# Block sums of w_out on one engine, and low parts of a weight and of a few rows moved off VectorE, in an attention and two-MoE kernel

## The chip, the cores and the metric

The kernel runs on one core of a Trainium2 chip. The metric is the device time of one execution in microseconds (us). The median of three runs of the kernel before is 1247.25 us (1245.92 to 1251.09).

## The reference

Attention over 4 batches of 8 heads, 576 positions and 64 columns, with a bias that a small network computes from the positions; its output, 2304 rows of 512, goes through a gated layer of width 1536 (the first MoE) and then through a squared-relu layer of width 2048 (the second MoE). All data are float32 or wider.

```python
scores = scale * np.matmul(q, k.transpose(0, 1, 3, 2))
...
return np.matmul(attn, v).astype(np.float32)

def _moe_ref(x, w_gate, w_val, w_out) -> np.ndarray:
    g = x @ w_gate
    silu = g * (1.0 / (1.0 + np.exp(-g)))
    val = x @ w_val
    return (silu * val @ w_out).astype(np.float32)

def _moe2_ref(x, w_in, w_out) -> np.ndarray:
    h = np.maximum(x @ w_in, 0.0)
    return (h * h @ w_out).astype(np.float32)
```

## The kernel before

Every product is made of float16 parts: a number is written as a high part and a low part, and three matmuls (high by high, high by low, low by high) stand for one. Making parts is the work of ScalarE, VectorE and GpSimd. `halves` (L194) does it for a scaled input in one of four ways. In way 0 ScalarE writes the high part and VectorE the low part (`minus`, L191). In way 1 GpSimd writes the high part (L197) and VectorE the low part. In way 2 ScalarE scales the input in place (L205) and copies the high part (L209), and GpSimd subtracts for the low part (`rest_of`, L220). The table `MIX` (L30) lists for each kind of work which ways take turns; `mixed(key)` deals out the next. `diff` (L1192) is a sum or difference on VectorE for 0 and on GpSimd otherwise, and `parts2` (L1195) makes a high part (way 0 VectorE, 1 ScalarE, 2 GpSimd) and then a low part with `diff`.

The 2304 rows are nine units of 256. The first MoE takes them one by one (`moe1`, m from 0 to 8): gate and value products for 12 slices of the width (L458), `th` (L466 to L469), then the output product (L481) and `out_y` (L490), which scales the two halves of 128 rows, splits them into a high and a low part in the tile `yh` and stores them to DRAM through SP's queue (L502). The second MoE reads them back transposed.

Beside the last units of the first MoE the weights of the second are prepared (`weights2`, L1236). `first` decodes columns 2 and 3 of w_in (columns 0 and 1 were done earlier), finds a scale for each, and calls `split` (L286) four times for each; `second` does the same for the 16 blocks of w_out (key "2"), with a norm on ScalarE (L361) in between.

The second MoE treats unit 0 alone (`plain`, L1386) and the others as four pairs (`hidden`, `outputs`). For a pair, the eight blocks of rows of w_out are multiplied by the seven-product scheme of Strassen in Winograd's form: seven products in place of eight, for which sums and differences of blocks are needed on both sides. The sums of the hidden rows are made by GpSimd in `hidden` (key "s", tile `zx`). Those of w_out's blocks are made once, by `combine(f)` (L1206) for f from 0 to 7: seven differences into the tile `w2t` (three of 128x512, four of 128x256; L1220 to L1226, dealt out by key "t" as two on VectorE, one on GpSimd), then a high part on ScalarE (key "c") and a low part on VectorE or GpSimd (key "d": 0, 1, 1) into `TS[f]`. All eight use the one buffer `w2t`. Blocks 0 to 2 are called at the end of `weights2`; block 3 in `plain` behind f = 1, 4 behind f = 3, 5 behind f = 5, 6 behind f = 7, and 7 in front of the output products (L1403), of which there are two for 128 rows each, 48 matmuls each, going through f from 0 to 7.

In `hidden`, TensorE makes two products of 12 matmuls for each f (L1375) into banks of a pool of five; ScalarE reads a bank with relu (L1380) and squares (L1384), GpSimd makes four sums, and `parts2` makes the parts, which `outputs` (L1434) multiplies (L1447). In `outputs`, sums of the products are kept in small tiles c1, u2, u4, u3 with two buffers each, in the pool `wk`.

The order of the instructions on each engine is not that of the program. A planner in the compiler simulates the engines with its own costs and lets each engine take, of what is ready, what comes first in the program; what stands under `high_priority` goes ahead. On the chip each engine keeps the order thus found. Two generators, attention with the weights and the first MoE, are interleaved by hand-set positions (`LEAD`, L37).

Of the kernel before, what the change touches and what calls it, by code (L numbers as in the profile page):

```python
# [10 lines left out]
F32 = mybir.dt.float32  # L11
# [4 lines left out]
AF = mybir.ActivationFunctionType  # L16
ALU = mybir.AluOpType
# [7 lines left out]
P = 128  # L25
# [4 lines left out]
MIX = {  # L30
# [4 lines left out]
}  # L35

# [39 lines left out]
def tile_attention_moe(  # L76
# [4 lines left out]
    nc = tc.nc  # L81
# [20 lines left out]
    st = {}  # L102
# [111 lines left out]
    def mixed(k):  # L214

        mix_n[k] = mix_n.get(k, -1) + 1
        return MIX[k][mix_n[k] % len(MIX[k])]

    def rest_of(out_, x, hi):
        nc.gpsimd.tensor_tensor(out=out_, in0=x, in1=hi, op=ALU.subtract)  # L220
# [65 lines left out]
    def split(ring, key, j, kc, sc):  # L286

        src = ring.whole(key, j, kc)
        hi, lo = [ring.parts(key, j, kc, l) for l in range(2)]
        halves(hi, lo, src, sc, mixed(key))  # L290

    def root_scale(m, mm):

# [126 lines left out]
    def junk_tile():  # L420
        return junk1
# [68 lines left out]
    def out_y(m, t, po, iu):  # L490
        ss = scr([P, 1], tag="yss")
        nc.scalar.activation(junk_tile()[:, 0:512], po, AF.Square, accum_out=ss)
        r = expo(ss, half=True)
        sy = scr([P, 1], tag="ysy")
        nc.vector.tensor_scalar(
            out=sy, in0=r[:, 1:2], scalar1=2.0 ** -50, scalar2=None, op0=ALU.mult)
        mul(ftok[:, 2 * m + t:2 * m + t + 1], r[:, 0:1], iu, 2.0 ** 49)
        yh = mw.tile([P, 2, DM], F16, tag="yh", name="yh", bufs=1)
        nc.scalar.activation(yh[:, 0, :], po, AF.Copy, scale=sy)
        nc.vector.scalar_tensor_tensor(  # L500
            out=yh[:, 1, :], in0=po, scalar=sy, in1=yh[:, 0, :], op0=ALU.mult, op1=ALU.subtract)
        nc.sync.dma_start(y_d[m][P * t:P * t + P, :], yh.rearrange("p l e -> p (l e)"))  # L502


# [701 lines left out]
    def combine(f):  # L1206

        q = st["w2r"].t.rearrange("p a b -> p (a b)").bitcast(F16).rearrange("p (s c) -> p s c", c=256)
        t = st["w2t"]
        tv = t.rearrange("p (a b c) -> p a b c", a=2, b=2)  # L1210
        t1, t2, t3, t4 = [t[:, 256 * i:256 * i + 256] for i in range(4)]
        a, b = 4 * (W2 + f), 4 * (W2 + 8 + f)

        def right(l):
            return q[:, a + 2 * l + 1:b + 2 * l + 2:32, :]

        def left(l):
            return q[:, a + 2 * l:a + 2 * l + 2, :]

        t13 = tv[:, :, 0, :]  # L1220
        diff(t13, right(0), left(0), mixed("t"))
        diff(t13, t13, right(1), mixed("t"), ALU.add)
        diff(t13, t13, left(1), mixed("t"))
        for x, c, y in ((t2, b + 1, t1), (t4, b, t2)):
            diff(x, q[:, c], y, mixed("t"))
            diff(x, x, q[:, c + 2], mixed("t"), ALU.add)  # L1226
        hi, lo = st["TS"][f]
        parts2(hi, lo, t, "c", "d")
# [7 lines left out]
    def weights2():  # L1236
        a_stack.close()
        w2p = ctx.enter_context(tc.tile_pool(name="w2p", bufs=2, side="right"))
        ps2 = ctx.enter_context(tc.tile_pool(name="ps2", bufs=5, space=PSUM))
        w2r = Ring(w2p.tile([P, 25, 512], F32, name="w2r", bufs=1), {  # L1240
            "w": lambda j, kc: (w2a, 4 * j + kc) if j < 2 else 4 * j - 8 + kc, "2": lambda j, kc: W2 + kc})
        st["w2p"], st["ps2"], st["w2r"] = w2p, ps2, w2r

        def mm2():
            return ps2.tile([P, 512], F32, tag="ph", name="mm2")

        w2s = w2p.tile([P, 3584], F32, name="w2s", bufs=1)
        sg2 = Stage(
            512, [w2s[:, 1024 * i:1024 * i + 1024].bitcast(I64) for i in range(3)],
            [w2s[:, 3072 + 256 * i:3328 + 256 * i].bitcast(BF16) for i in range(2)])  # L1250
        yield from first(w2r, {"w": w2i}, range(2, 4), block_rows, sg2, 3, mm2)
        kappa = []
        for j in range(4):
            kap = keep()
            mul(kap, st["iw", j], st["iw", j], KR)
            kappa.append(kap)
        yield from second(w2r, "2", NF2, w2o, kappa, sg2, 3, mm2, True)
        new = w2p.tile([P, 4096], F16, name="w2c", bufs=1)

        st["w2t"] = w2p.tile([P, 1024], F32, name="w2t", bufs=1)  # L1260
        w2h, wrh, w2sh = [t.rearrange("p a b -> p (a b)").bitcast(F16) for t in (
            w2r.t, wr.t, w2s.rearrange("p (a b) -> p a b", a=7))]
        rooms2 = [w2sh[:, 1024 * i:1024 * i + 1024] for i in range(7)] + [w2h[:, 1024 * 24:1024 * 25]] + [
            new[:, 1024 * i:1024 * i + 1024] for i in range(4)] + [
            wrh[:, 1024 * i:1024 * i + 1024] for i in (4, 5, 6, 36)]
        st["TS"] = [rooms2[2 * f:2 * f + 2] for f in range(8)]
        st["HS"] = [wrh[:, int(1024 * o):int(1024 * o) + 3584] for o in (7.5, 11, 15, 18.5, 22, 25.5, 29, 32.5)]
        st["yt"] = wrh[:, 0:4096]
        for f in range(3):
            if f == 1:  # L1270
                yield ("gv", 8)
                yt_load((0,))
            combine(f)
            yield 3.0
# [70 lines left out]


    wk = ctx.enter_context(tc.tile_pool(name="wk", bufs=2, side="left"))
    fac = res.tile([P, 18], F32, name="fac")
    nc.vector.tensor_scalar(out=fac, in0=ftok, scalar1=st["G1"], scalar2=None, op0=ALU.mult)
    mul(fac, fac, fac)  # L1350
# [83 lines left out]
    def outputs(us):  # L1434
        n = 256 * len(us)
        nh = n // 2
        last_bank = mm2()
        for t in range(nh // P):
            banks = [mm2(), mm2(), mm2()] if t else [ma(), mm(), mm()]
            (p1, p2), (p6, p7), (p5, p3) = [[bk[:, 256 * i:256 * i + 256] for i in range(2)] for bk in banks]  # L1440
            p4 = last_bank[:, 256 * t:256 * t + 256]

            def product(po, a, b, fs=range(8)):
                for f in fs:
                    for k, (l, wl) in enumerate(((0, 0), (0, 1), (1, 0))):
                        o = nh * (a - 1 + 7 * l) + P * t
                        nc.tensor.matmul(  # L1447
                            po, HS[f][:, o:o + P], right_of(f, wl, b),
                            start=f == 0 and k == 0, stop=f == 7 and k == 2)

            def sums(name):
                return wk.tile([P, 256], F32, tag=name, name=name)

            def add(name, x, y):
                o = sums(name)
                nc.vector.tensor_tensor(out=o, in0=x, in1=y, op=ALU.add)
                return o

            def row(j, h, src, other):

                i = nh * (1 - h) + P * t
                u, tt = us[i // 256], i % 256 // P
                sc = fac[:, 2 * u + tt:2 * u + tt + 1]
                o = obs[h][:, 256 * j:256 * j + 256]
                nc.vector.tensor_tensor(out=o, in0=src, in1=other, op=ALU.add)
                nc.scalar.activation(o, o, AF.Copy, scale=sc)

            obs = [wk.tile([P, DM], F32, tag="ob", name="ob", bufs=3) for _ in range(2)]
            early_, late_ = (range(6), range(6, 8)) if t == 0 else (range(8), ())
            for fs in (early_, late_):  # L1470
                for po, a, b in ((p1, A11, B11), (p6, S2, T2), (p5, S1, T1)):
                    product(po, a, b, fs)
            c1 = sums("c1")
            nc.scalar.copy(c1, p1)
            u2 = add("u2", p6, c1)
            u4 = add("u4", p5, u2)
            product(p7, S3, T3)
            u3 = add("u3", p7, u2)
            row(1, 1, p5, u3)
            product(p2, A12, B21)  # L1480
            row(0, 0, p2, c1)
            product(p3, S4, B22)
            row(1, 0, p3, u4)
            product(p4, A22, T4)
            row(0, 1, p4, u3)
            for h in range(2):
                i = nh * (1 - h) + P * t
                for p0, np_, r0 in out_rows(us[i // 256], i % 256 // P):
                    nc.sync.dma_start(out[r0:r0 + np_, :], obs[h][p0:p0 + np_, :])
# [37 lines left out]
```

## Time and profile before

| | |
|---|---|
| median of three runs | 1247.25 us |
| the profiled execution | 1241.6 us, its span 1239.8 us |
| mean granted TensorE clock | 0.954 of full speed |
| TensorE (PE) busy | 1099.7 us, 89% |
| VectorE (DVE) busy | 782.3 us, 63% |
| ScalarE (ACT) busy | 669.9 us, 54% |
| GpSimd (POOL) busy | 642.3 us, 52% |

A busy share says how long an engine worked in the span. A window shows the same for a stretch, with the granted clock (1.00 is 2.4 GHz) and the share of DMA. In a row of groups or of a timeline stand line, engine, operation, output and inputs with their shapes, and in brackets or behind a bar how long the engine stood idle before it and who ended that. A wait list adds such idle times up. L1193 is the line of `diff`, so its instructions are told apart by tile: w2t is a block sum of w_out, zx a sum of the hidden rows, wr a part of them (or of a block sum, wr<-w2t).

### The profile page before, as it was taken

To read this page: it belongs to the slowest core of one execution; us is meant where nothing else is said; L and a number is where in the kernel's file an instruction comes from. 1 tells how busy PE (TensorE), PEld (TensorE's weight loads), DVE (VectorE), ACT (ScalarE), POOL (GpSimd) and SP (SyncE) were. 2 spreads that over 40 slices of the span, in tenths; PEclk is the share of its full clock that TensorE was granted. 3 is DMA by queue.
4 is the path that set the end of the run, shared out by engine and by line. 5 is a ranking of instruction groups with operands and counts; after the bars stand their busy time and mean duration, and the time that the engine had idled before them with its cause. 6 is when DMAs were issued, how large, how long until landed. Compare 5 with 4: busy or idle time off the path is not lost. (4 is left out here: it accounts for less than half of the span.)

```text
span 1239.8 us, 27146 instructions
## 1 busy us (share of the span) xinstructions
PE 1099.7 (89%) x10478; PEld 811.3 (65%) x10478; DVE 782.3 (63%) x1866; ACT 669.9 (54%) x1350; POOL 642.3 (52%) x811
## 2 busy tenths in 40 slices
PE   2587799998678889999997999979998899999998
PEld 2566788686467578686774767556743756848657
DVE  5989857887676666666565745884757335153361
ACT  3567767557566566566563543365635245163451
POOL 2433213279768697778694462235567236062360
PEclk9779799999879999999999999989999899999999
DMA  8957543219999999998989994650201101002001
GB/s 220 266 134 208 177 132 87 50 58 201 220 214 209 217 218 169 230 184 170 182 170 247 240 228 129 213 176 10 43 17 23 30 18 35 35 1 52 19 1 35
DMA packets 278078, 163.20 MB, mean 132 GB/s; under 512 B 233276, under 2 KB 246588, under 8 KB 277948
## 3 DMA queue, kind: packets, MB, share of 16 engines
q1 hardware_dynamic: 277948, 161.46, 55.9%
q8 instruction: 82, 1.34, 0.5%
q14 instruction: 48, 0.39, 0.1%
HBM read 92.13 MB, written 19.48 MB: 90 GB/s over the span
## 5 line engine op out<-in xcount | busy, mean ns | idle before, releaser
L458 PEld LDWEIGHTS <-wr 128*128 128x128 f16 x2592 | 253.4, 100 | 50.7 <-issue 14.9
L1193 POOL TENSOR_TENSOR zx<-zx 128x256 f32<-128x256 f32 x128 | 123.3, 974 | 150.1 <-ACT zx L1384 145.4
L458 PE MATMUL mm<-xT,wr 128*128 128x256 f16 x1536 | 185.5, 276 | 7.9 <-DVE yh L500 3.4
L220 POOL TENSOR_TENSOR pt<-s,pt 128x512 f16<-128x512 f32 x224 | 173.1, 796 | 30.4 <-ACT pt L836 27.8
L1447 PEld LDWEIGHTS <-wr 128*128 128x128 f16 x1344 | 132.1, 99 | 23.8 <-ACT wr L1200 3.5
L220 POOL TENSOR_TENSOR zx<-th,zx 128x256 f16<-128x256 f32 x108 | 82.5, 765 | 123.7 <-ACT zx L443 117.6
L481 PE MATMUL mm<-wr,zx 128*128 128x512 f16 x612 | 143.1, 381 | 1.5 <-DVE sc L828 1.1
L1193 DVE TENSOR_TENSOR wr<-zx,wr 128x768 f16<-128x768 f32 (+2 forms) x72 | 93.3, 1302 | 66.6 <-ACT wr L1200 65.6
L821 DVE CUSTOM_DVE_ANT_0 s<-qk,room 128x576 f32<-128x576 f32 x144 | 107.8, 749 | 40.8 <-PE qk L812 24.0
L829 ACT ACTIVATE s<-s,sc 128x576 f32<-128x576 f32 x112 | 85.6, 771 | 56.1 <-DVE sc L828 48.9
L458 PE MATMUL mm<-zx,wr 128*128 128x256 f16 x864 | 105.1, 279 | 2.8 <-DVE th L469 1.5
L1375 PE MATMUL mm<-wr,room 128*128 128x512 f16 (+1 forms) x480 | 101.3, 361 | 4.6 <-ACT zx L1380 4.5
L481 PEld LDWEIGHTS <-zx 128*128 128x128 f16 x648 | 60.3, 98 | 66.4 <-issue 3.5
L604 DVE TENSOR_TENSOR scrap<-scrap,room 128x1024 f16<-128x1024 f16 (+1 forms) x108 | 85.1, 801 | 24.3 <-PE ma L643 20.6
L1375 PE MATMUL mm<-wr,w2r 128*128 128x512 f16 (+1 forms) x480 | 100.0, 358 | 0.0
L620 POOL TENSOR_TENSOR scrap<-scrap 128x256 f32<-128x256 f32 (+1 forms) x90 | 64.1, 712 | 64.7 <-ACT scrap L619 56.5
L874 PE MATMUL av<-vp,pT 128*128 128x65 f16 (+3 forms) x1792 | 70.8, 197 | 26.9 <-DMA pT<-pt 23.9
L874 PEld LDWEIGHTS <-pT 128*128 128x128 f16 (+1 forms) x1792 | 61.7, 103 | 42.3 <-DMA pT<-pt 33.0
L1375 PEld LDWEIGHTS <-room 128*128 128x128 f16 x480 | 47.2, 98 | 52.1 <-issue 7.5
L643 PEld LDWEIGHTS <-scrap 128*128 128x128 f16 x1440 | 60.0, 105 | 27.5 <-issue 11.9
L1375 PEld LDWEIGHTS <-w2r 128*128 128x128 f16 x480 | 47.0, 98 | 46.6
L812 PE MATMUL qk<-kp,qT 128*128 128x288 f16 x384 | 64.1, 293 | 11.4 <-DMA kp<-kT_d 6.1
(273 smaller groups left out, 2093.3 us busy)
## 6 DMA issues: line engine op xcount, KB each, us to landing
kp<-kT_d SPq DMA_DIRECT2D x64, 288.0 KB, 3.3
vp<-v_d SPq DMA_DIRECT2D x48, 325.0 KB, 3.6
w2s<-in_moe_w_out_dram SPq DMA_DIRECT2D x16, 512.0 KB, 4.1
wr<-in_moe_w_gate_dram SPq DMA_DIRECT2D x24, 256.0 KB, 4.8
wst<-in_moe_w_out_dram SPq DMA_DIRECT2D x12, 512.0 KB, 3.6
wr<-in_moe_w_val_dram SPq DMA_DIRECT2D x24, 256.0 KB, 4.2
v_d<-vp SPq DMA_DIRECT2D x16, 325.0 KB, 2.9
y_d<-yh SPq DMA_DIRECT2D x18, 256.0 KB, 3.4
```

The source lines that it names most:

```text
L220: nc.gpsimd.tensor_tensor(out=out_, in0=x, in1=hi, op=ALU.subtract)
L458: nc.tensor.matmul(pg[:, 256 * gi:256 * gi + 256], wr.parts(key, f // 4, cc, wl, P * (f % 4), P), mov(xl, cc), start=k == 0, stop=k == 11)
L481: nc.tensor.matmul(po, zall[:, f, zl, P * t:P * t + P], wr.parts("o", 0, f, wl), start=k == 0, stop=k == 3 * NF1 - 1)
L604: nc.vector.tensor_tensor(out=m[:, :, ni * e:ni * e + ni], in0=block(kb, i0, ni), in1=th, op=ALU.is_gt)
L620: nc.gpsimd.tensor_tensor(out=tmp[r], in0=tmp[r], in1=xb, op=ALU.mult)
L812: nc.tensor.matmul(pq[:, j, 0:288], qT[:, 2 * (n % 4) + s, :], kts[0][:, js], start=s == 0, stop=s == 1)
L821: nc.vector.tensor_tensor_reduce(out=s.rearrange("p (a j) -> p a j", a=2), in0=pq[:, :, 0:288], in1=bias[:, n].rearrange("p (a j) -> p a j ...
L829: nc.scalar.activation(s, s, AF.Exp, bias=nm, scale=-1.0)
L874: nc.tensor.matmul(av[r, slot, 0:cn], pT[:, 5 * l + c, r], vs[e][c][:, c0:c0 + cn], start=m == 0, stop=m == 13)
L1193: (nc.gpsimd if how else nc.vector).tensor_tensor(out=out_, in0=a, in1=b, op=op)
L1375: nc.tensor.matmul(ph[:, :n], w2r.parts("w", g // 4, cc, wl, P * (g % 4), P), yt[:, 4 * yl + cc, :], start=m == 0, stop=m == 11)
L1447: nc.tensor.matmul(po, HS[f][:, o:o + P], right_of(f, wl, b), start=f == 0 and k == 0, stop=f == 7 and k == 2)
```

## The change

It does four things. Key "t" deals out only VectorE, so that all 56 differences of `combine` are made there. `combine` takes its buffer from a list that goes round: one buffer, as before, in `weights2`, and three from `plain` on, the two halves of a new tile `four` in the pool `wk` and the old one; the small tiles of `outputs` go into the halves of `four` in turn, in place of their own. `split` uses way 2 for columns 2 and 3 of w_in, where ways 2, 0, 1 took turns over the eight calls. And for m = 7 and 8 `out_y` has ScalarE write the scaled rows in float32 to a scratch tile, ScalarE copy the high part, and GpSimd subtract for the low part.

```diff
-    "t": (0, 0, 1), "c": (1,), "d": (0, 1, 1), "q": (0,), "s": (1,), "a": (1, 1, 0),
+    "t": (0,), "c": (1,), "d": (0, 1, 1), "q": (0,), "s": (1,), "a": (1, 1, 0),
...
-        halves(hi, lo, src, sc, mixed(key))
+        halves(hi, lo, src, sc, 2 if key == "w" and j > 1 else mixed(key))
...
-        nc.scalar.activation(yh[:, 0, :], po, AF.Copy, scale=sy)
-        nc.vector.scalar_tensor_tensor(
-            out=yh[:, 1, :], in0=po, scalar=sy, in1=yh[:, 0, :], op0=ALU.mult, op1=ALU.subtract)
+        if m < 7:
+            nc.scalar.activation(yh[:, 0, :], po, AF.Copy, scale=sy)
+            nc.vector.scalar_tensor_tensor(
+                out=yh[:, 1, :], in0=po, scalar=sy, in1=yh[:, 0, :], op0=ALU.mult, op1=ALU.subtract)
+        else:
+            y = junk_tile().bitcast(F32)
+            nc.scalar.activation(y, po, AF.Copy, scale=sy)
+            nc.scalar.copy(yh[:, 0, :], y)
+            rest_of(yh[:, 1, :], y, yh[:, 0, :])
...
-        t = st["w2t"]
+        t = st["w2t"][0]
+        st["w2t"].append(st["w2t"].pop(0))
...
-        st["w2t"] = w2p.tile([P, 1024], F32, name="w2t", bufs=1)
+        st["w2t"] = [w2p.tile([P, 1024], F32, name="w2t", bufs=1)]
...
+    four = wk.tile([P, 2048], F32, name="four", bufs=1)
+    st["w2t"] = [four[:, 0:1024], four[:, 1024:2048]] + st["w2t"]
...
-            def sums(name):
-                return wk.tile([P, 256], F32, tag=name, name=name)
+            def sums(i):
+                return four[:, 1024 * (t % 2) + 256 * i:1024 * (t % 2) + 256 * i + 256]
...
-            c1 = sums("c1")
+            c1 = sums(0)
             nc.scalar.copy(c1, p1)
-            u2 = add("u2", p6, c1)
-            u4 = add("u4", p5, u2)
+            u2 = add(1, p6, c1)
+            u4 = add(2, p5, u2)
             product(p7, S3, T3)
-            u3 = add("u3", p7, u2)
+            u3 = add(3, p7, u2)
```

## Rows read from the trace of the kernel before

**Rows 1.** Windows of two pairs (engines' busy us, instructions, clock, DMA)

```profile
908.34:1001.34 93.00, 83.02 (x530) 52.60 (x529) 48.13 (x52) 36.31 (x56) 46.05 (x43) 0.94 0.08 21
1001.34:1079.46 78.12, 78.12 (x530) 51.65 (x528) 31.41 (x35) 34.03 (x53) 30.33 (x32) 1.00 0.10 28
```

**Rows 2.** Stage window: the last rows of the first MoE

```profile
805.80:840.00 34.20, 26.43 (x198) 20.98 (x197) 30.21 (x74) 22.36 (x56) 11.31 (x11) 0.85 0.51 161
```

**Rows 3.** TensorE's waits after 800 us (total us, times, longest)

```profile
PE mm L1375 <- ACT zx L1380: 4.5, 2, 3.2
PE ma L458 <- DVE th L469: 4.3, 1, 4.3
PE ma L1447 <- ACT wr L1200: 3.2, 1, 3.2
PE mm L131 <- DVE sc L495: 3.0, 1, 3.0
```

**Rows 4.** Window of the instructions on tile w2t alone

```profile
863.40:951.50 88.10, 31.14 (x41) 8.35 (x8) 30.59 (x23) 0.99 0.10 25
```

**Rows 5.** Waits between 868 and 1002 us, all engines

```profile
POOL w2t L1193 <- DVE w2t L1193: 16.9, 13, 3.7
```

**Rows 6.** ScalarE's timeline, first pair (start, us, instruction, idle before)

```profile
913.72 0.60 ACT L1380 ACTIVATE zx<-mm 128x512 f32<-128x512 f32 x1 [1.33 <-PE mm L1375]
918.38 1.04 ACT L1200 CAST w2c<-w2t 128x1024 f16<-128x1024 f32 x1 [4.06 <-POOL w2t L1193]
```

**Rows 7.** Tile w2t on VectorE (ns min/median/max), one timeline row

```profile
L1193 DVE TENSOR_TENSOR w2t<-w2r,w2t x11: 414/426/1367, 867.3 to 946.3; 128x256 f32<-128x256 f16 x11
L1193 DVE TENSOR_TENSOR w2t<-w2r x6: 676/692/1207, 863.5 to 937.7; 128x512 f32<-128x512 f16 x6
L1193 DVE TENSOR_TENSOR wr<-w2t,wr x1: 1218/1218/1218, 935.1 to 935.1; 128x1024 f16<-128x1024 f32 x1
946.26 0.93 DVE L1193 TENSOR_TENSOR w2t<-w2r,w2t 128x256 f32<-128x256 f16 x1 [0.56 <-POOL w2t L1193]
```

**Rows 8.** Groups on VectorE, 860 to 955 us (busy us, mean ns)

```profile
L1193 DVE TENSOR_TENSOR w2t<-w2t,w2r 128x512 f32<-128x512 f32 x10 | 8.4, 839 | 6.1 <-POOL w2t L1193 5.9
L1193 DVE TENSOR_TENSOR w2t<-w2t,w2r 128x256 f32<-128x256 f32 x11 | 6.9, 628 | 3.4 <-POOL w2t L1193 3.3
L1193 DVE TENSOR_TENSOR w2t<-w2r,w2t 128x256 f32<-128x256 f16 x11 | 6.6, 601 | 5.9 <-POOL w2t L1193 5.8
L1193 DVE TENSOR_TENSOR w2t<-w2r 128x512 f32<-128x512 f16 x6 | 5.2, 859 | 3.9 <-POOL w2s L1193 3.8
```

**Rows 9.** Tile yh: its stores, first and last issue, time to landing

```profile
L502 SPq DMA_DIRECT2D y_d<-yh x18: 337/343/934, 248.4 to 874.4; - x18
DMA to landing us min/median/max: 2.0/3.4/6.6
```

**Rows 10.** TensorE's timeline: the plain unit's products

```profile
887.62 20.88 PE L1403 MATMUL mm<-w2r,wr 128*128 128x512 f16 x96
```

**Rows 11.** Windows around 878 us; the first of tile wr alone

```profile
878.00:894.00 16.00, 16.00 (x119) 3.04 (x31) 6.97 (x9) 2.46 (x4) 0.00 (x0) 1.00 0.34 67
870.00:878.00 8.00, 8.00 (x76) 7.16 (x75) 7.65 (x15) 6.59 (x17) 5.35 (x5) 1.00 0.08 33
```

**Rows 12.** Groups of VectorE and ScalarE, 795 to 840 us

```profile
L191 DVE SCALAR_TENSOR_TENSOR w2r<-w2r,keep 128x512 f16<-128x512 f32 x5 | 4.1, 826 | 0.6 <-POOL w2r L197 0.6
L500 DVE SCALAR_TENSOR_TENSOR yh<-mm,sc,yh 128x512 f16<-128x512 f32 x2 | 1.5, 746 | 0.0
L262 DVE TENSOR_SCALAR w2r<-w2s 128x512 int32<-128x512 int32 x14 | 7.7, 552 | 4.4 <-DMA w2s<-in_moe_w_out_dram 4.3
811.90 0.75 DVE L191 SCALAR_TENSOR_TENSOR w2r<-w2r,keep 128x512 f16<-128x512 f32 x1 [0.59 <-POOL w2r L197]
L205 ACT ACTIVATE w2r<-w2r,keep 128x512 f32<-128x512 f32 x3 | 2.1, 716 | 4.0 <-DVE keep L296 4.0
L209 ACT CAST w2r<-w2r 128x512 f16<-128x512 f32 x3 | 1.8, 611 | 0.1
```

More of the change, by code (lines that the diff above doesn't have):

```diff
@@ L1449, in product, with add @@
                             start=f == 0 and k == 0, stop=f == 7 and k == 2)
-            def sums(name):
-                return wk.tile([P, 256], F32, tag=name, name=name)
-            def add(name, x, y):
-                o = sums(name)
+            def sums(i):
+                return four[:, 1024 * (t % 2) + 256 * i:1024 * (t % 2) + 256 * i + 256]
+            def add(i, x, y):
+                o = sums(i)
                 nc.vector.tensor_tensor(out=o, in0=x, in1=y, op=ALU.add)
```

## The prediction

> **What bounds the kernel now.** I read the slices of the page first, then the stage windows, then TensorE's waits, then the timelines of the stages with holes. TensorE is the busiest engine by far, so a change on the others can only pay where it stands still or runs at a lowered clock. The second pair of units of the second MoE shows a stretch with no loss: 78.12 us, TensorE busy in all of it, granted clock 1.00. The first pair needs 93.00 us for the same 530 matmuls: busy 83.02 of it, at a mean clock of 0.94 [rows 1]. That is 93.00 - 78.12 = 14.9 us, of which 93.00 - 83.02 = 10.0 is idle and 4.9 clock. A second stretch with loss is 805.8 to 840, the last rows of the first MoE beside the decoding of the second MoE's weights: TensorE is busy 26.43 of 34.2 us at a clock of 0.85, so 7.8 us are idle [rows 2]. In TensorE's list of waits after 800 us both stand out: 4.5 us for ScalarE's relu (L1380) and 3.2 us for a high part of the hidden rows in the first pair, 4.3 us for VectorE's th (L469) and 3.0 us put down to L495 in the other [rows 3]. Everything else of the 1239.8 us is out of reach of this change: before 800 us it alters nothing that runs.
>
> Why is the first pair late? The sums of w_out's blocks (combine) go on into it: 41 VectorE and 23 GpSimd instructions on w2t lie between 863.4 and 951.5, 31.1 and 30.6 us busy [rows 4]. They share one buffer, so a block starts only when the low part of the last one is done, and inside a block VectorE and GpSimd take turns: GpSimd waited 13 times, 16.9 us, for VectorE's w2t [rows 5]. Because each engine takes its instructions in order, the pair's own work stands behind them: ScalarE, having read one bank at 913.72, sat 4.06 us for GpSimd's w2t before its next instruction [rows 6], and the banks that it should empty are the ones TensorE then waits for.
>
> **The change part by part.**
> *Sums on VectorE, three buffers.* All 56 differences go to VectorE; 18 leave GpSimd (its 23 on w2t less five low parts). A block has three of 512 columns and four of 256. With GpSimd quiet one takes 0.69 and 0.43 us (the medians), beside GpSimd 1.21 and 0.93 [rows 7]; the means over the stretch are (8.4 + 5.2)/16 = 0.85 and (6.9 + 6.6)/22 = 0.61 [rows 8]. So a block costs VectorE 3 x 0.69 + 4 x 0.43 = 3.8 us at best, 5.0 at the means, 7.4 at worst, and needs no other engine until its high part. Blocks 3 and 4 get the two halves of the new tile, 5 the old buffer, 6 and 7 the halves again. The new tile lies where the first MoE's buffers lay, so it is free when the last y is stored: issued at 874.4, 3.4 to land, about 878 [rows 9]. From then on VectorE can run ahead through blocks 3 to 7 instead of following the low parts. Five blocks at the mean are 25 us, beside TensorE's plain products, 20.9 us from 887.62 [rows 10]; they should be over when or shortly after the first pair begins at about 908. What is then late next in that pair? Nothing new: its own work is that of the later pairs, which runs without a hole. I take the whole 14.9 us. Bounds: 0, if the blocks still run into the pair, to 14.9.
>
> The price is on the plain unit in front of it. VectorE serves what comes first in the program: block 3 stands before f = 2, block 4 before f = 4, block 5 before f = 6. TensorE reaches f = 7 of its first plain product at 887.62 + 7/8 of half of 20.88 = 896.75 [rows 10], and VectorE must by then have done, from 878, its plain work on the hidden rows (6.97 us between 878 and 894) [rows 11], one low part of w2 (0.83) [rows 12], one low part of a block (1.22) [rows 7], and blocks 2 to 5 if 5 really goes ahead. With four blocks of cost c the row f = 7 is 878 + 6.97 + 0.83 + 1.22 + 4c - 896.75 = 4c - 9.7 us late: 5.4 at best, 10.3 at the means, 19.7 at worst. With three (block 5 must wait for block 2's low part on GpSimd, and slips behind): 1.6, 5.3, 12.3. GpSimd will be quieter here than it was, since 18 differences leave it, but it keeps most of the low parts. I take 5.0 us of idle time, which is three blocks at the mean or four at best. Bounds: a gain or loss of 0 (TensorE is fed in another order) to a loss of 19.7.
>
> *Low parts of w_in's second half.* Eight blocks were split in three ways; three had both parts off VectorE already. Five VectorE instructions go (4.1 us) and ScalarE then has eight scalings (0.716) and eight copies (0.611) in place of three, three, and three scaled copies taken at 0.716 as well: 8 x 1.327 - 3 x 1.327 - 3 x 0.716 = 4.5 us more [rows 12]. GpSimd gets five more low parts and loses two high parts.
> *Rows of the units m = 7 and 8.* Four VectorE instructions of 0.75 us go, two of them in this stretch (1.5 us) [rows 12]; each is replaced by one more ScalarE copy and a GpSimd difference, and the bank is free after ScalarE's first instruction. The other two belong to m = 8, at a time when TensorE is full; the 1.5 us that they give VectorE ahead of 878 go into its start at 878.
> Together 5.6 us leave VectorE between 795 and 840 and 5.7 go to ScalarE. In front of TensorE's 4.3 us wait (th stands behind the decoding on VectorE) lie two of the low parts, one y and a 0.59 us wait for GpSimd: 0.75 + 0.75 + 0.75 + 0.59 = 2.8 us [rows 12]. But ScalarE's tanh, which th needs, then stands behind one scaling and two copies of the split more and one copy of y: 0.716 + 3 x 0.611 = 2.5 us. The decoding also waits for DMA (4.3 us over the stretch) [rows 12], so VectorE would meet part of what it gains there. On SP's queue the store of y stands ahead of loads; ScalarE and GpSimd finish y about when VectorE's turn used to come, so nothing moves. The 3.0 us wait lies before the first removed instruction and stays. Bounds: -2.5 (ScalarE leads) to +2.8, and with luck in the order all 7.8 us and their clock. I take +2.0.
>
> **The sum.** 14.9 - 5.0 + 2.0 = 11.9 us. The profiled execution took 1241.6 us (span 1239.8), so 1229.7 for one like it. The median of the runs shown is 1247.25, 5.65 above that execution; I set the gain off from the median: 1247.25 - 11.9 = 1235.4, say 1235.
>
> **A rule weighed.** VectorE's difference of 256 columns takes 0.426 us in the median and up to 1.367 [rows 7]. The Trainium skill, SBUF — State Buffer, Who interferes with whom, gives a reason: an instruction of VectorE with two SBUF inputs and a GpSimd instruction that reads SBUF exclude each other, and the loser waits for the whole instruction. The Trainium skill, Perfetto Trace Analysis, Optimizing Scalar/DVE Operations, draws from it that shifting work between these two engines "might not help". By the strict rule every difference would cost the long price; by the rows, half of them ran at the short one although both engines were at work.
>
> **The rivals.**
> *1. The plain products wait longer.* All four blocks go ahead of f = 7 at the mean price: 10.3 us idle, and a clock that falls behind it as in the first pair (4.9 on 10.0 of idle), at most 5 more. For: VectorE was already busy 7.65 of the 8 us before 878 [rows 11]. Against: block 5's buffer. Taking 12.6 for both: 14.9 + 2.0 - 12.6 = 4.3 us of gain, 1243.
> *2. The buffers decouple nothing.* The blocks still run one by one, since the high part goes through ScalarE's queue and two of three low parts through GpSimd's, each behind work of its own, or since the order of the program changes with the costs. Then only the turns between VectorE and GpSimd go and the first pair keeps its holes: 1247. Against: with three buffers VectorE need not wait for either.
> *3. VectorE becomes the bound (the other side).* Its differences cost the long price from 878 on, because GpSimd's low parts lie beside nearly all of them. The plain product is 19.7 us late, the first pair gains its 14.9, and ScalarE's load eats the +2.0: 4.8 us slower, 1252. It decides from a block of (14.9 + 9.7)/4 = 6.2 us on, halfway between the mean and the worst. The port rule of the Trainium skill's page SBUF — State Buffer speaks for it.
> *4. The first stretch clears too.* If TensorE's 4.3 us wait and the clock behind it go with the 2.8 us on VectorE, and the plain products lose nothing: 14.9 + 2.0 + 5 = 22, 1225.
>
> **How the numbers follow.** Forecast 0.50, its own range 1229 to 1241; rival 1 0.20, rival 2 0.08, rival 3 0.12, rival 4 0.10. The range 1224 to 1248 leaves out rival 3 and the rim of the others. A measurement here can tell about 0.5%, 6.2 us, from no change: faster means below 1241.0, slower above 1253.5. Faster: nearly all of the forecast (0.48), rival 4, a third of rival 1 and a little of rival 2: 0.67. Slower: rival 3's upper half and a little of the mishaps of the order: 0.10. The same: 0.23.
>
> **What would show it.** Right: the first pair's 530 matmuls in about 78 us at clock 1.00; on GpSimd only the five low parts left of its work on w2t; the last difference before 915 instead of 947; L1380 and L1447 gone from TensorE's waits there; TensorE's plain products with some 5 us of idle time, waiting for VectorE's low parts. Wrong: differences still running beyond 930, plain products more than 10 us late, or 805.8 to 840 longer than before with TensorE waiting for ScalarE's tanh.

## The result, and the profile after

The changed kernel takes 1235.97 us (median of 6 runs, 1228.09 to 1246.81), the kernel before 1246.63 (6 runs): a ratio of 0.9889, 95% interval 0.9850 to 0.9928. A ratio leaves out slow runs, those over 1.5% above the fastest of their kernel (1246.81 here, 1244.61 of sums_block_lows further down), which the medians keep, so it is not the quotient of the medians. The forecast was 1235. The profiled execution took 1236.04 us (span 1234.2, clock 0.962).

`diff` is L1199 now, `parts2`'s high part on ScalarE L1206, the product of `hidden` L1384, its relu L1389, the plain products L1412, those of `outputs` L1456, the store of y L508. The windows of four stages (as in [rows 1]: length, then busy us and instructions of TensorE, its weight loads, VectorE, ScalarE and GpSimd, then clock, DMA share and GB/s): from the output product of m = 7 to the plain products (the decoding stage, in what follows), the plain products, the first pair, the second pair.

```profile
794.75:895.57 100.82, 89.76 (x649) 64.14 (x649) 74.38 (x169) 61.46 (x140) 45.60 (x44) 0.95 0.32 97
895.57:916.29 20.72, 20.72 (x98) 9.37 (x96) 20.62 (x37) 8.77 (x15) 4.72 (x2) 1.00 0.30 64
916.29:995.32 79.03, 78.47 (x529) 51.52 (x528) 35.56 (x42) 34.84 (x55) 35.59 (x34) 1.00 0.10 24
995.32:1073.44 78.12, 78.12 (x529) 51.46 (x527) 30.77 (x35) 34.06 (x53) 30.73 (x32) 1.00 0.11 28
```

The decoding stage in the kernel before:

```profile
789.45:887.62 98.17, 90.40 (x649) 64.13 (x649) 72.98 (x169) 56.07 (x130) 43.20 (x42) 0.95 0.31 98
```

The first pair, 93.00 us with 83.02 busy in [rows 1], now takes 79.03 with 78.47 busy at clock 1.00, nearly what the second takes. The plain products run without a hole in 20.72 us. The decoding stage is 2.65 us longer. TensorE's waits after 790 us (as in [rows 3]) say the same:

```profile
PE mm L131 <- DVE sc L495: 4.5, 1, 4.5
PE mm L169 <- DVE sc L166: 3.8, 1, 3.8
PE ma L458 <- DVE th L469: 1.9, 1, 1.9
PE mm L1384 <- ACT zx L1389: 0.9, 1, 0.9
```

The 4.5 us for relu and the 3.2 us for a high part [rows 3] are gone; the three waits at the top belong to the decoding stage and add up to 10.2 us, where [rows 3] had 4.3 + 3.0. The 0.9 us for relu lies in front of the plain products, not in the pair. Tile w2t, which is now one of three buffers (ns min/median/max, first and last start):

```profile
L1199 DVE TENSOR_TENSOR w2t<-w2t,w2r x16: 411/552/1532, 869.0 to 919.2; 128x512 f32<-128x512 f32 x8, 128x256 f32<-128x256 f32 x8
L1199 DVE TENSOR_TENSOR w2t<-w2r x4: 679/683/685, 868.3 to 913.0; 128x512 f32<-128x512 f16 x4
L1199 POOL TENSOR_TENSOR w2s<-w2t,w2s x2: 2132/2352/2571, 887.8 to 906.8; 128x1024 f16<-128x1024 f32 x2
L1199 POOL TENSOR_TENSOR w2c<-w2t,w2c x1: 2133/2133/2133, 921.7 to 921.7; 128x1024 f16<-128x1024 f32 x1
```

GpSimd has only low parts left on it, and the last difference starts at 919.2, 3 us into the first pair, where it started at 946.3 [rows 7], 38 us into it.

### The profile page after: what moved, and what is told of

It reads as the page before. It is cut to its first block, busy times and chain, and to the rows that moved or that the text cites. A ratio compares the mean times of both kernels' runs of the same rounds, so it can differ in the third digit from the quotient of the medians.

```text
span 1234.2 us, 27159 instructions
## 1 busy us (share of the span) xinstructions
PE 1093.6 (89%) x10478; PEld 806.7 (65%) x10478; DVE 774.3 (63%) x1875; ACT 676.1 (55%) x1361; POOL 629.6 (51%) x800
## 4 chain that ended last, share of the span: by engine, by line
PE 45%; DMA 16%; DVE 9%; POOL 8%; ACT 4%; issue 4%; SPq 1%; POOLq 0%; ACTq 0%; DVEq 0%
PE mm L1384 11%; PE mm L458 10%; PE mm L1456 10%; DMA pT<-pt 4%; PE mm L481 3%; POOL pt L220 2%; POOL zx L1199 2%; DMA qT<-qs 2%; PE av L880 2%; DMA scrap<-in_moe_w_in_dram 2%; PE mm L1412 2%; PE ma L1456 1%; PE qk L818 1%; DMA w2s<-in_moe_w_out_dram 1%; DMA w2s<-in_moe_w_in_dram 1%
## 5 line engine op out<-in xcount | busy, mean ns | idle before, releaser
L1199 POOL TENSOR_TENSOR zx<-zx 128x256 f32<-128x256 f32 x128 | 123.2, 972 | 152.3 <-ACT zx L1393 147.2
L1456 PEld LDWEIGHTS <-wr 128*128 128x128 f16 x1344 | 131.1, 98 | 17.7 <-DVE wr L1204 0.8
L220 POOL TENSOR_TENSOR zx<-th,zx 128x256 f16<-128x256 f32 x108 | 79.7, 739 | 118.5 <-ACT zx L443 114.7
L1199 DVE TENSOR_TENSOR wr<-zx,wr 128x768 f16<-128x768 f32 (+1 forms) x72 | 91.0, 1270 | 72.7 <-ACT wr L1206 71.7
L1384 PE MATMUL mm<-wr,w2r 128*128 128x512 f16 (+1 forms) x480 | 99.9, 358 | 0.9 <-ACT zx L1389 0.9
L1384 PE MATMUL mm<-wr,room 128*128 128x512 f16 (+1 forms) x480 | 100.1, 358 | 0.0
L1384 PEld LDWEIGHTS <-w2r 128*128 128x128 f16 x480 | 47.0, 98 | 47.4 <-issue 1.0
L1384 PEld LDWEIGHTS <-room 128*128 128x128 f16 x480 | 47.0, 98 | 46.0
L818 PEld LDWEIGHTS <-qT 128*128 128x128 f16 x512 | 48.8, 101 | 40.0 <-issue 15.2
```

What stands on the lines that cost most here:

```text
L818: nc.tensor.matmul(pq[:, j, 0:288], qT[:, 2 * (n % 4) + s, :], kts[0][:, js], start=s == 0, stop=s == 1)
L1199: (nc.gpsimd if how else nc.vector).tensor_tensor(out=out_, in0=a, in1=b, op=op)
L1384: nc.tensor.matmul(ph[:, :n], w2r.parts("w", g // 4, cc, wl, P * (g % 4), P), yt[:, 4 * yl + cc, :], start=m == 0, stop=m == 11)
L1456: nc.tensor.matmul(po, HS[f][:, o:o + P], right_of(f, wl, b), start=f == 0 and k == 0, stop=f == 7 and k == 2)
```

## The experiments

All times by stage are read from TensorE's timeline of one profiled execution each; the median is of 4 to 12 runs, the ratio is against runs of the kernel before on the same chip (median 1245.57 for the first four experiments, 1248.38 for the next four, 1246.29 for the last two). Line numbers shift with the edits: `diff` is L1193 or L1199, the plain products stand between L1403 and L1415. In the stage up to m = 7 each engine has the same instructions in the same order in every kernel, so its spread of 13 us is one between executions; no experiment is judged by it.

| us | to m = 7's output | decoding stage | plain products | first pair | rest | median | ratio, 95% |
|---|---|---|---|---|---|---|---|
| before | 789.5 | 98.2 | 20.7 | 92.8 | 238.6 | 1246.63 | |
| after | 794.8 | 100.8 | 20.7 | 79.0 | 238.9 | 1235.97 | 0.9889 (0.9850 to 0.9928) |
| sums_only | 798.6 | 99.3 | 22.5 | 79.4 | 238.6 | 1236.48 | 0.9914 (0.9892 to 0.9936) |
| lows_only | 793.2 | 101.4 | 20.7 | 90.1 | 238.6 | 1247.14 | 1.0015 (0.9998 to 1.0033) |
| buffers_only | 793.9 | 102.2 | 26.5 | 78.7 | 238.6 | 1242.17 | 0.9973 (0.9952 to 0.9993) |
| vector_only | 791.7 | 98.2 | 20.7 | 88.7 | 238.7 | 1239.87 | 0.9961 (0.9933 to 0.9989) |
| sums_and_split | 790.2 | 101.3 | 20.7 | 78.1 | 238.6 | 1233.58 | 0.9889 (0.9861 to 0.9917) |
| sums_and_rows | 798.0 | 101.4 | 20.7 | 79.8 | 238.6 | 1235.15 | 0.9899 (0.9868 to 0.9931) |
| gpsimd_loaded | 793.3 | 106.7 | 23.4 | 90.4 | 238.7 | 1253.64 | 1.0054 (1.0033 to 1.0076) |
| block_lows_vector | 794.7 | 101.6 | 20.7 | 78.1 | 238.7 | 1234.24 | 0.9885 (0.9850 to 0.9921) |
| sums_block_lows | 802.5 | 97.8 | 20.7 | 78.1 | 238.7 | 1233.35 | 0.9891 (0.9865 to 0.9918) |
| changed_again | 790.0 | 100.2 | 20.7 | 79.1 | 238.6 | 1237.74 | 0.9937 (0.9915 to 0.9959) |

### sums_only: the sums without the moved low parts

```diff
(against the change)
-        halves(hi, lo, src, sc, 2 if key == "w" and j > 1 else mixed(key))
+        halves(hi, lo, src, sc, mixed(key))
...
(out_y as before)
```

> The block sums as changed (all on VectorE, three buffers), the low parts of w_in and of m = 7, 8 as before. Theory: the gain is the first pair's, so it falls from 93.0 to about 79 us here too, and the stretch of the last first-MoE rows is as before (the changed kernel lost some 1.8 us there): 1246.6 - 14 + 1 = about 1233.5, a ratio of 0.9895, 2 us under the changed kernel. Rival: the low parts that left VectorE made the room for the sums; then the plain products or the first pair show waits for VectorE again (first pair 82 or more) and the time is 1238 or above.

The sums alone carry the gain: 1236.48 us, about the time of the whole change and not 2 us under it. Here the wait that the prediction priced does occur, at 1.60 us (TensorE, then VectorE and GpSimd, from their timelines):

```profile
909.16 11.40 PE L1406 MATMUL mm<-w2r,wr 128*128 128x512 f16 x52 [1.60 <-DVE wr L1193]
```

```profile
903.55 3.14 DVE L1193 TENSOR_TENSOR w2r<-four,w2s 128x1024 f16<-128x1024 f32 x1
...
908.42 0.68 DVE L1193 TENSOR_TENSOR wr<-zx,wr 128x512 f16<-128x512 f32 x1
```

```profile
903.06 2.55 POOL L1193 TENSOR_TENSOR w2c<-four,w2c 128x1024 f16<-128x1024 f32 x1 [0.59 <-ACT w2c L1200]
```

The low part for f = 7 stands behind a block's low part, which takes 3.14 us while GpSimd works and 1.22 in the kernel after. A low part of the plain unit itself, at 900.82, takes 2.20 us beside the GpSimd low part before that one.

### lows_only: the moved low parts without the sums

```diff
(against the kernel before)
-        halves(hi, lo, src, sc, mixed(key))
+        halves(hi, lo, src, sc, 2 if key == "w" and j > 1 else mixed(key))
...
(out_y as in the change; combine, "t" and the small sums as before)
```

> Only the low parts move (w_in's second half and the rows of m = 7, 8); block sums as before, one buffer, two engines. Theory: first pair stays at 93 us, the stretch of the last first-MoE rows loses 0 to 3 us: 1246.6 to 1249.5. Rival (the prediction's own +2.0): 1244.6.

Between 0.02% faster and 0.33% slower: no gain. The decoding stage is 3.2 us longer, the first pair 2.7 shorter.

### buffers_only: three buffers, the differences dealt out as before

```diff
(as sums_only, and)
-    "t": (0,), "c": (1,), "d": (0, 1, 1),
+    "t": (0, 0, 1), "c": (1,), "d": (0, 1, 1),
```

> Three buffers, but the differences dealt out two on VectorE, one on GpSimd as before; low parts as before. Theory: both steps are needed, since the engines still take turns inside a block and GpSimd's share (about 1.1 us each) runs on into the pair: first pair about 85 us, 1240. Rival A (the buffer was all): first pair 79, 1233.5, as with the sums on VectorE. Rival B (the engine was all): 93, 1246.6.

The pair is cured (78.7, where 85 was expected), but 3.4 us is all that the kernel gains, as the plain products pay for it (windows of the plain products and the pair, then TensorE's waits):

```profile
896.14:922.65 26.51, 22.93 (x99) 9.59 (x96) 18.97 (x22) 9.50 (x17) 16.29 (x12) 0.94 0.22 50
922.65:1001.36 78.71, 78.46 (x529) 51.50 (x528) 34.50 (x39) 33.85 (x53) 34.80 (x35) 1.00 0.09 24
```

```profile
PE mm L1406 <- DVE wr L1193: 3.1, 2, 2.3
PE mm L1378 <- ACT zx L1383: 2.7, 1, 2.7
```

GpSimd is busy 16.29 of the 26.51 us, VectorE 18.97: each block still goes back and forth between them, now ahead of the plain unit's own low parts.

### vector_only: the differences on VectorE, one buffer

```diff
(against the kernel before)
-    "t": (0, 0, 1), "c": (1,), "d": (0, 1, 1),
+    "t": (0,), "c": (1,), "d": (0, 1, 1),
```

> All differences on VectorE, but one buffer; low parts as before. A block then takes 3.8 to 5.0 us of differences, 1.05 of ScalarE and 2.13 (or 1.22) of the low part one after the other, about 7.5 us; eight of them from 864 end near 925 in place of 951. Theory: first pair about 82 us, 1236. Rival A (the buffer was all): 93, 1246.6. Rival B (the engine was all): 79, 1233.5.

The other half: the plain products stay at 20.7, and the pair keeps most of its loss (88.7, where 82 was expected). The waits for relu are gone; those of `outputs` for parts of the hidden rows are left. Each block still waits for the low part of the one before it, and ScalarE, which also makes the pair's high parts, for each block (TensorE's waits; ScalarE's timeline):

```profile
PE ma L1447 <- ACT wr L1200: 3.8, 1, 3.8
PE ma L1447 <- DVE wr L1193: 2.8, 2, 1.9
```

```profile
915.03 1.04 ACT L1200 CAST w2c<-w2t 128x1024 f16<-128x1024 f32 x1 [3.56 <-DVE w2t L1193]
```

### sums_and_split and sums_and_rows: each half of the moved low parts with the sums

```diff
(sums_and_split: the change, but out_y as before)
(sums_and_rows: the change, but the four calls of split as before)
-        halves(hi, lo, src, sc, 2 if key == "w" and j > 1 else mixed(key))
+        halves(hi, lo, src, sc, mixed(key))
```

> Block sums as changed, w_in's second half split in way 2 as changed, the rows of m = 7 and 8 as before. In single profiles the sums alone left a 1.6 us wait in the plain products (22.5 us for them, 20.7 with the whole change). Theory: the two 0.75 us of y before 890 on VectorE make that difference, and the split only loads ScalarE: plain products about 22.5, first pair 79, the stretch of the last first-MoE rows 1 to 2 us longer than with the sums alone: 1237.5 to 1238.5. Rival: the split is what helps, plain products 20.7, 1234.

> Block sums as changed, the rows of m = 7 and 8 as changed, w_in's second half split as before. Theory: plain products 20.7, first pair 79, and the stretch of the last first-MoE rows as before (no more scalings on ScalarE): 1233.5, 1 to 2 us under the whole change. Rival: plain products 22.5 or more, 1236.5.

Neither can be told from sums_only by its median. The plain products take 20.7 us in both, so the 1.60 us wait of sums_only goes with either half, and not with the rows of m = 7 and 8 alone as was expected. By the profiles either half alone makes the decoding stage as long as both do: 101.3 and 101.4, where the rows of m = 7 and 8 were expected to leave it as before.

### gpsimd_loaded: the change with GpSimd kept busy

For f = 3 to 7, four additions on a scratch tile are given to GpSimd behind the differences; they change nothing of the output.

```diff
(against the change)
+        if f > 2:
+            for _ in range(4):
+                diff(junk1.bitcast(F32), junk1.bitcast(F32), junk1.bitcast(F32), 1)
```

> The changed kernel with four useless 128x512 GpSimd differences on an idle scratch tile behind each of blocks 3 to 7 (20 in all, about 1.15 us each), so that GpSimd reads SBUF while VectorE makes the sums. Theory (a difference is dear when GpSimd runs beside it): the differences of blocks 3 to 5 go from about 3.4 us a block to 5.0 to 7.4, the plain row f = 7 comes 5 to 12 us later and the plain products wait 4 to 10 us; first pair still about 79 to 81: 1240 to 1247. Rival (the length of a difference has nothing to do with GpSimd): 1236, no wait.

This is the rival on the other side, made true: 1253.64 us, slower than before, and above the 1240 to 1247 expected, since the pair is not spared. VectorE and GpSimd (timelines), and TensorE's waits:

```profile
893.98 1.52 DVE L1199 TENSOR_TENSOR w2t<-w2r 128x512 f32<-128x512 f16 x1
895.43 1.52 DVE L1199 TENSOR_TENSOR wr<-zx,wr 128x512 f16<-128x512 f32 x1
...
905.55 0.68 DVE L1199 TENSOR_TENSOR w2t<-w2t,w2r 128x512 f32<-128x512 f32 x1
```

```profile
889.40 15.68 POOL L1199 TENSOR_TENSOR junk<-junk 128x512 f32<-128x512 f32 x11
```

```profile
PE mm L1387 <- ACT zx L1392: 4.3, 3, 3.0
...
PE ma L1459 <- ACT wr L1206: 3.1, 1, 3.1
...
PE mm L1415 <- DVE wr L1199: 1.7, 2, 0.9
```

While GpSimd's eleven additions run (1.43 us each), a difference of 512 columns takes 1.52 us; the first one after them takes 0.68. Sums and low parts are late on both sides of the plain products, and the pair is back at 90.4. The additions also put off GpSimd's own low parts (block 4's starts at 913.27, 13.3 us into the plain products, where it was 9.1), so the time lost is not the price of the longer differences alone.

### block_lows_vector: the change with the blocks' low parts on VectorE too

```diff
(against the change)
-    "t": (0,), "c": (1,), "d": (0, 1, 1),
+    "t": (0,), "c": (1,), "d": (0,),
```

> The changed kernel with all eight low parts of the block sums on VectorE (three before), so GpSimd is silent between 890 and 920. Theory (as for the loaded GpSimd): no difference above 0.8 us is left there, five low parts of 1.22 us come to VectorE, 6.1 us in a stretch where it was full; since the long differences cost it about 5 us, the sums end at the same time, plain products 20.7 to 22, first pair 79: 1235 to 1238. Rival: VectorE is the bound now, the sums end 6 us later and run into the pair: 1240 or more.

A window over the plain products:

```profile
890.00:920.00 30.00, 30.00 (x170) 16.39 (x168) 29.71 (x55) 15.99 (x30) 0.00 (x0) 1.00 0.22 51
```

GpSimd does nothing there, no difference takes longer than 0.68 us, and the last one starts at 915.8 in place of 919.2. VectorE, with more to do, is full for 29.71 of 30 us and TensorE still never waits. Against the kernel after it is 1.7 us, within the intervals.

### sums_block_lows and changed_again: the version the runs pointed to, beside the change

```diff
(sums_block_lows: sums_only, and)
-    "t": (0,), "c": (1,), "d": (0, 1, 1),
+    "t": (0,), "c": (1,), "d": (0,),
(changed_again: the change as it is)
```

> A candidate to beat the changed kernel: the block sums as changed, all eight low parts of the block sums on VectorE as well, and the low parts of w_in and of m = 7, 8 as before the change. Theory: the 1.6 us wait of the plain products with the sums alone came from a low part that GpSimd made 3.1 us long, so it goes (plain products 20.7, first pair 78.1), and the stretch from the output product of m = 7 to the plain products keeps its 98 to 99.5 us, since nothing is added to ScalarE there: some 2 to 3 us under the changed kernel, 1232 to 1234. Rival: the low parts are needed on top, plain products 22 or more or first pair 80 or more, and the time is that of the changed kernel or above.

> The changed kernel as it is, for a comparison on the same chip: a ratio of 0.989 to the kernel before; first pair 78 to 79.5, plain products 20.7. What lies before the output product of m = 7 has the same order in all kernels here, so its length (789 to 799 us so far) tells what single profiles differ by.

The window of sums_block_lows, decoding stage:

```profile
802.46:900.21 97.75, 89.46 (x652) 63.58 (x649) 77.72 (x182) 55.95 (x130) 34.74 (x36) 0.97 0.32 99
```

On one chip it is 1233.35 against 1237.74 us, 4.4 us faster. Its three stages add up to 97.8 + 20.7 + 78.1 = 196.6 us, against 200.0 for changed_again and 200.5 for the kernel after. The two intervals of the ratio, up to 0.9918 and from 0.9915, just overlap, so it is likely, and not certain, that it beats the change.

## Why the prediction was right, step by step

The sum, 14.9 - 5.0 + 2.0 = 11.9 us of gain, came close to the 10.7 of the medians. One term was right, one was mis-sized and one had the wrong sign. The errors of these two, +5.0 and -4.6, nearly cancel: that the sum came so close is luck. By the ratios the gain is 13.8 us (9.0 to 18.7), and 7.9 (5.1 to 10.6) in changed_again, on another chip. By stages: 13.8 in the first pair, 0.0 in the plain products, -2.6 in the decoding stage, -0.3 in the rest, together 10.9; the stretch up to m = 7, which nothing alters, took 5.3 us longer in this pair of executions.

**The first pair, +14.9: right, 13.8 measured.** What was said of it is what is seen: TensorE full at clock 1.00, GpSimd left with low parts only, the waits for relu and for a high part gone; the last difference, at 919, misses the mark of 915, in an execution whose pair begins 8 us later. The small tiles in the halves of `four` show no price: the second pair takes 78.12 us before and after. Which part does it: the buffers alone bring the pair to 78.7, the engine alone to 88.7. So the second rival, that the buffers decouple nothing, is refuted by buffers_only. But neither is worth much alone: 3.4 and 5.7 us by the medians against 9.1 for both in sums_only. The buffers move the holes from the pair into the plain products, and the single engine then takes most of them away.

**The price on the plain unit, -5.0: mis-sized, 0 there and 0.9 just ahead.** The step said that VectorE's low part for f = 7 would be 4c - 9.7 us late, or 3c - 9.7 if block 5 slips behind, with c = 5.0 at the means. VectorE's timeline after (the halves of `four` hold blocks 3 and 4 here, and w2t holds block 2, told by the tiles that their low parts go to):

```profile
890.85 1.29 DVE L1199 TENSOR_TENSOR four<-w2r 128x512 f32<-128x512 f16 x2
892.05 0.69 DVE L1199 TENSOR_TENSOR w2t<-w2r 128x512 f32<-128x512 f16 x1
892.65 0.69 DVE L1199 TENSOR_TENSOR wr<-zx,wr 128x512 f16<-128x512 f32 x1
...
902.70 0.68 DVE L1199 TENSOR_TENSOR wr<-zx,wr 128x512 f16<-128x512 f32 x1
903.30 0.42 DVE L1199 TENSOR_TENSOR w2t<-w2t,w2r 128x256 f32<-128x256 f32 x1
903.64 1.22 DVE L1199 TENSOR_TENSOR w2r<-four,w2s 128x1024 f16<-128x1024 f32 x1
```

The low part for f = 7 ends at 903.38, and TensorE gets to f = 7 at 895.57 + 7/8 of half of 20.88 = 904.70: it is 1.3 us early, not 5 late. The number of blocks was right: 2, 3 and 4 lie ahead of it, and block 5 starts at 913.0 only, behind block 2's low part on GpSimd, from 906.8 (rows of w2t in the section on the result). Their cost was wrong. Between 890.85 and 903.64 lie 21 differences, three blocks, and six pieces of the plain unit's own. Five of these start 0.60 or 0.61 us before the next instruction, one (a copy) 0.34, some 3.4 us in all, which leaves 9.4, or 3.1 us a block. By the step's own sum 3 x 3.1 - 9.7 = -0.4: not late. 3.1 is under the lower bound of 3.8, since the rows' durations overlap: 0.69 us long, they start 0.60 apart. And GpSimd did not work beside them, so the mean and worst prices did not apply (its timeline):

```profile
887.79 2.13 POOL L1199 TENSOR_TENSOR w2s<-w2t,w2s 128x1024 f16<-128x1024 f32 x1
904.65 2.19 POOL L1199 TENSOR_TENSOR w2c<-four,w2c 128x1024 f16<-128x1024 f32 x1 [14.72 <-ACT w2c L1206]
```

"VectorE serves what comes first in the program" was not seen as I used it: the three blocks and the plain unit's low parts are interleaved, three differences to one low part. That helps the earlier f; the low part for f = 7 still stands behind 20 of the 21 differences. The new tile was not early either (tile yh, ns min/median/max, first and last issue):

```profile
L508 SPq DMA_DIRECT2D y_d<-yh x18: 332/346/1091, 249.9 to 887.9; - x18
```

The last store of y is issued 7.7 us before the plain products, where 874.4 [rows 9] was 13.2 before them. The margin is thin: sums_only pays 1.60 us where low parts on GpSimd fall beside low parts on VectorE, buffers_only 3.1.

**The moved low parts, +2.0: wrong in sign, -2.6, with that 0.9 in it.** Two steps failed. The first is that the 3.0 us wait "lies before the first removed instruction and stays": it grew to 4.5. It ends with VectorE's L332, and from m = 7's output product to there VectorE has the same 42 instructions in the same order in every kernel (windows of that stretch before and after; GpSimd and VectorE after):

```profile
789.45:809.49 20.04, 17.28 (x97) 8.24 (x96) 17.24 (x42) 7.27 (x16) 3.90 (x4) 0.99 0.65 202
794.75:816.34 21.59, 17.28 (x97) 8.24 (x96) 18.31 (x42) 9.00 (x20) 4.44 (x5) 1.00 0.71 207
```

```profile
812.07 1.15 POOL L220 TENSOR_TENSOR w2r<-w2r 128x512 f16<-128x512 f32 x1 [9.99 <-PE ma L458]
814.65 1.15 POOL L220 TENSOR_TENSOR w2r<-w2r 128x512 f16<-128x512 f32 x1 [1.43 <-ACT w2r L209]
```

```profile
812.13 1.65 DVE L265 SCALAR_TENSOR_TENSOR w2r<-w2s,w2r 128x512 int32<-128x512 int32 x1
...
814.76 1.06 DVE L187 SCALAR_TENSOR_TENSOR ftok<-sc,ux 128x1 f32<-128x1 f32 x1
```

L265 takes 0.68 us and L187 0.14 where GpSimd is silent. With the split moved GpSimd has two low parts of w_in in that stretch in place of one. VectorE is busy there for 17.9 to 18.4 us in the six kernels with the split moved, and for 16.6 to 17.2 in the six without; TensorE's wait is 3.5 to 4.6 us, 4.2 in the mean, against 2.4 to 3.9 and 2.8. So some 1.3 us of the loss is VectorE's other work made longer by the low parts that were given to GpSimd.

The second is that 2.8 us leave VectorE in front of TensorE's next wait. The prediction asked whether ScalarE's tanh would eat them. It does not (ScalarE, VectorE and GpSimd after; then VectorE before):

```profile
821.73 0.46 ACT L466 ACTIVATE th<-ma,ux 128x256 f32<-128x256 f32 x1
```

```profile
816.34 0.15 DVE L332 TENSOR_REDUCE sc<-mm 128x1 f32<-128x4 f32 x1
...
821.26 1.03 DVE L262 TENSOR_SCALAR w2r<-w2s 128x512 int32<-128x512 int32 x1 [1.39 <-DMA w2s<-in_moe_w_out_dram]
...
824.38 1.32 DVE L262 TENSOR_SCALAR w2r<-w2s 128x512 int32<-128x512 int32 x1
...
826.35 0.13 DVE L166 TENSOR_SCALAR sc<-sc 1x1 f32<-1x1 f32 x1
...
827.51 0.41 DVE L467 SCALAR_TENSOR_TENSOR th<-th,ma 128x256 f32<-128x256 f32 x1
```

```profile
820.85 1.15 POOL L220 TENSOR_TENSOR w2r<-w2r 128x512 f16<-128x512 f32 x1
824.06 1.36 POOL L220 TENSOR_TENSOR w2r<-w2r 128x512 f16<-128x512 f32 x1 [2.06 <-ACT w2r L209]
```

```profile
809.49 0.15 DVE L332 TENSOR_REDUCE sc<-mm 128x1 f32<-128x4 f32 x1
...
819.07 0.40 DVE L467 SCALAR_TENSOR_TENSOR th<-th,ma 128x256 f32<-128x256 f32 x1
...
820.32 0.13 DVE L166 TENSOR_SCALAR sc<-sc 1x1 f32<-1x1 f32 x1
```

tanh starts at 821.73, but VectorE comes to th at 827.51 only. What TensorE waits for is VectorE's chain of small instructions for a weight's scale, from L332 to the last L166. The chain takes 826.35 - 816.34 = 10.0 us with the moved parts, 820.32 - 809.49 = 10.8 before, so VectorE's 2.8 us became 0.8. The order in which VectorE takes its work was made anew. One decoding instruction more lies in the chain, twelve in place of eleven, and two of them, beside low parts on GpSimd, take 1.03 and 1.32 us, where 0.41 is the common length. In the order before, th (L467) stood inside that chain, at 819.07; now it stands behind it, and TensorE stops at the chain (3.8 us) and then at th (1.9).

That the moved parts lengthen the stage is a comparison over kernels: 97.8 to 99.3 in the four without them (before, sums_only, vector_only, sums_block_lows), 100.2 to 101.6 in the six with one or both (after and its repeat, lows_only, sums_and_split, sums_and_rows, block_lows_vector); the means are 98.4 and 101.1. buffers_only, at 102.2 without them, has its 2.7 us wait there; gpsimd_loaded's load lies there. The medians, whose intervals are some 4 to 10 us wide, neither confirm nor exclude 2.7 us; what they do exclude, through lows_only, is a gain of over 0.3 us. Up to m = 8's output product the kernels part more cleanly: 62.3 to 63.9 us in the five without moved parts, 64.9 to 67.1 in the seven with them, 3.1 us between the means. Where the split is moved, the first wait is 1.3 us of these, and up to 12 more matmuls of 256 columns, done here and not later, are up to 1.4, by the 24 that take 2.78. sums_and_rows has next to none of either, and why it takes 66.1 us stays open. That the new place of the chain costs anything is argued, not shown: in sums_only, with the order of before, the three waits add up to 9.7 us too.

**The other rivals.** Longer waits in the plain products did not come in the change but did in buffers_only. The bound on VectorE is real in gpsimd_loaded and was not met, because GpSimd, with 18 differences less, stood idle for 14.72 us beside the three blocks that decide. The first stretch did not clear.

**A rule weighed, again.** The differences next to a busy GpSimd took 1.52 us, next to a silent one 0.68. The Trainium skill, SBUF — State Buffer, Who interferes with whom, says that a VectorE instruction with two SBUF inputs contends with a GpSimd instruction that reads SBUF; gpsimd_loaded agrees, and block_lows_vector shows the same instructions free of it. It spoke for the third rival and, read the other way, for the change.

## What to carry to other kernels

Before pricing work moved from one engine to its neighbour, ask whether the neighbour still works in that stretch: the price beside a busy engine can be twice the price beside a silent one (1.52 us against 0.68 here), and the move itself decides which holds. The same goes for work given to the neighbour: it can lengthen what the first engine keeps. More buffers and one engine for the whole chain may each move a hole only; look at the stage in front of the one that is cured. Instructions taken off an engine in a planned order are no time won for what waits on it until one knows what the planner puts in their place.

## What the runs showed that I had not expected

The same 790 us of instructions, in the same order on each engine, took 789.5 to 802.5 us in the profiled executions, more than this change is worth. Stages read from one trace are therefore compared by their own length and not by where they start.
